# Attention decode kernel: K and V in units of eight heads and rows of 65536 B instead of units of two heads and rows of 49152 B

## The chip, the cores and the metric

The kernel runs on one core of one Trainium2 chip. The metric is the device time of one execution in microseconds, the median of three runs. Here and below the engines are called as the profile calls them: PE (matrix multiplication), PEld (its weight loads), DVE (vector engine), ACT (activation engine), POOL, and SP, which issues the large DMA transfers. A DMA transfer goes in rows, one contiguous run for each of the 128 partitions of on-chip memory.

## The reference

Two independent attention blocks, A and B, each decode one token for two batch entries with 32 heads of 192 dimensions over 8192 cached tokens. All arrays are bfloat16.

```python
def _A_ref(x, k_cache, v_cache, wq, wo):          # _B_ref computes the same
    q = (x @ wq).reshape(B, Sq, Hq, Dh).transpose(0, 2, 1, 3)
    scores = jnp.einsum("bhqd,bhkd->bhqk", q, k) * (Dh ** -0.5)
    p = _softmax(scores, axis=-1)
    o = jnp.einsum("bhqk,bhkd->bhqd", p, v)
    return o.transpose(0, 2, 1, 3).reshape(B, Sq, Hq * Dh) @ wo
return jnp.concatenate([a, b], axis=-1)
```

K and V of both blocks have 2 x 2 x 2 x 32 x 8192 x 192 elements of two bytes, 805.3 MB. The weights wq and wo of both blocks add 31.5 MB. Every byte is read once, and each is used in about one multiplication.

## The kernel before

The work is cut into **64 units** of two heads of one batch entry of one block (`NU`, L134). A unit's K is one DMA load of 6.29 MB (`ld_kv`, L264): partitions 0 to 63 hold the first head, 64 to 127 the second, 128 tokens on each partition, 49152 B in one row. A unit's V is another such load. SP issues them in the order of `loads` (L213): K of unit 0, then K of unit 1, V of unit 0, K of unit 2, V of unit 1 and so on. They go in turn into three buffers (`NBUF`, L137), so load i waits until the data of load i-3 has been used up (`done`, L485). For K that is the unit's last multiplication on DVE, for V its last matmul. Beside the three buffers, two small ones (`prod`, L183) hold products.

**Queries.** At the start PE multiplies x by wq for one pair of heads after the other (`pe_q`, L353), with x spread over 64 partitions for each batch entry, so that each query comes out copied to the 64 partitions that need it. DVE and ACT move them to `qall`, where the queries of all 64 units lie (L279 to L286).

**Scores.** A unit's K is taken in four pieces of 32 tokens. DVE multiplies a piece by the unit's query into a product buffer (`dve_mul`, L288). PE adds groups of 16 dimensions by twelve matmuls with the identity (`pe_sum`, L363), and DVE adds the 16 partial sums that are left (`dve_red`, L293). Then DVE takes each partition's maximum (L296), POOL the maximum over the partitions (`pool_ar`, L270), ACT makes the bias of it and the exponentials with their sums (`act_nb`, `act_exp`).

**Output of a unit.** PE multiplies the exponentials with V, 64 matmuls with two tokens each (`pe_pv`, L348), in the program's order after the sums of the next unit. DVE and ACT divide by the sum and put the result back into `qall` (L304 to L314).

**The order on each engine** is fixed by the slot and the number given to `put` (L423, L440 to L461); inside a loop over three units nothing moves. On DVE the first multiplication of unit 1 stands ahead of unit 0's last reduction (L443). **At the end** `pe_turn` brings the outputs into the layout of the projection, block A's while the last unit still runs, and `pe_out` multiplies with wo, which SP loads after the last V into buffers that are free by then (`pieces`, L227).

Of the kernel before, what the change touches and what calls it, by code (L numbers as in the profile page):

```python
# [5 lines left out]
ALU = mybir.AluOpType  # L6
# [110 lines left out]

def build_kernel(nc, blocks, out):
# [4 lines left out]
    T = Sk // 64  # L123
    TC = 32
    NCH = T // TC
    TJ = T // 2
# [4 lines left out]
    PPB = Hn // 2  # L131
    UPB = PPB * B
    NP = NBLK * PPB
    NU = NP * B  # L134
    LASTU = NU - 1
    scale = float(Dh) ** -0.5
    NBUF = 3  # L137
    MP = 34
    JB = 16
    QW = 2 * Dh  # L140
    BUFE = T * Dh
    PRODE = TC * Dh
    WR = Hn * Dh // 128
    GP = Dh // WR
    HP = 32

    with ExitStack() as es:
# [4 lines left out]
        rc = [sb(f"rc{i}", [2, 1], F32) for i in range(3)]  # L152
        o_hi = sb("o_hi", [2, Dh], F32)
        ones = sb("ones", [128, 1], F32)
        big = sb("big", [128, NBUF * BUFE + 2 * PRODE], BF16)
        qall = sb("qall", [128, NU, Dh], BF16)
        pb = [sb(f"pb{i}", [128, 2 * T], BF16) for i in range(3)]
        actd = sb("actd", [128, 2], F32)
        xw = sb("xw", [128, NBLK * DC * 128 + D], BF16)
        sc = [sb(f"sc{i}", [128, T], F32) for i in range(3)]  # L160
        mp = [sb(f"mp{i}", [128, 2], F32) for i in range(3)]
        mg = [sb(f"mg{i}", [128, 2], F32) for i in range(3)]
        nb = [sb(f"nb{i}", [128, 1], F32) for i in range(3)]
        rs = [sb(f"rs{i}", [128, 2], F32) for i in range(3)]
        ident = sb("ident", [128, 128], BF16)
        tri = sb("tri", [HP, HP + 1], BF16)
        place = sb("place", [2, 256], BF16)
        o_sum = sb("o_sum", [2, Dh], F32)
        oT = [sb(f"oT{k}", [128, WR, B], BF16) for k in range(NBLK)]
        out_sb = sb("out_sb", [HP + B, D], BF16)  # L170
        first = sb("first", [16, 128], BF16)

        ops = [ps(f"ops{i}", [128, 512], F32) for i in range(3)]
        scps = [ps(f"scps{i}", [128, TC, DG], F32) for i in range(3)]
        outps = ps("outps", [128, 512], F32)
        oTps = ps("oTps", [128, 512], F32)
        qbank = [t[:].rearrange("p a b -> p (a b)") for t in scps]
        oacc = [outps[:], qbank[(LASTU * NCH + 1) % 3]]
        qps = qbank + [outps[:]]
        NQ = len(qps)  # L180

        kv = [big[:, i * BUFE:(i + 1) * BUFE].rearrange("p (t d) -> p t d", d=Dh) for i in range(NBUF)]
        prod = [big[:, NBUF * BUFE + i * PRODE:NBUF * BUFE + (i + 1) * PRODE].rearrange("p (t d) -> p t d", d=Dh)  # L183
                for i in range(2)]
        WQE = DC * Hn * Dh
        wq_off = [BUFE, BUFE + WQE]
        assert BUFE + 2 * WQE == NBUF * BUFE + 2 * PRODE
        wq_t = [big[:, o:o + WQE].rearrange("p (c n) -> p c n", c=DC) for o in wq_off]

        XBE = NBLK * DC * 128  # L190
        xbc = xw[:, 0:XBE].rearrange("p (k c m) -> p k c m", k=NBLK, c=DC)
        x4 = xw[0:NBLK * B, XBE:XBE + D]

# [3 lines left out]
        S_act = _Stream("act", sem("s_act"), reg)  # L197
        S_dve = _Stream("dve", sem("s_dve"), reg)
        S_pool = _Stream("pool", sem("s_pool"), reg)
# [7 lines left out]
        wq_cut = [[(0, WQ0), (WQ0, DC * Hn * Dh)], [(0, DC * Hn * Dh)]]  # L207
# [3 lines left out]
        dsem(("first",))  # L211
# [6 lines left out]
        bcount = [0] * NBUF  # L218
        for i, (kind, u) in enumerate(loads):
            buf[kind, u] = i % NBUF  # L220
            bcount[i % NBUF] += 1
            reg[(kind, u)] = (bsem[i % NBUF], 16 * bcount[i % NBUF])

        bk, b62, b63 = buf["k", LASTU], buf["v", LASTU - 1], buf["v", LASTU]
        assert (bk, b62, b63) == (2, 0, 1)
        woA, wo0, wo1 = bk * BUFE, b62 * BUFE, b63 * BUFE
        pieces = []  # L227
        for blk, rows, off, w in ((0, (WR,), woA, [("s", LASTU, NCH - 1)]), (1, (29,), wo0, [("pv", LASTU - 1)]),
                                  (1, (11, 5, 2, 1), wo1, [("pv", LASTU)])):
            r = 29 if off == wo1 else 0  # L230
            for n in rows:
                pieces.append((blk, r, r + n, off, w))
                off, r, w = off + n * D, r + n, []
            assert r == (29 if off == wo0 + 29 * D else WR)
        NA = 0
        assert 29 * D <= BUFE and woA + WR * D <= NBUF * BUFE + 2 * PRODE
        for n in range(len(pieces)):
            dsem(("wo", n))

        def key(name, *idx):  # L240
            return (name,) + tuple(idx)

        def back(name, u, c, n):
            i = u * NCH + c - n
            return (name, i // NCH, i % NCH) if i >= 0 else None

# [17 lines left out]
        def ld_kv(kind, u):  # L264
            hp, b = u // B, u % B
            blk, h = hp // PPB, 2 * (hp % PPB)
            src = blocks[blk][kind][b, h:h + 2].rearrange("s (p t) d -> (s p) t d", p=64)
            return dma(kv[buf[kind, u]], src, (kind, u))

        def pool_ar(u):  # L270
            return lambda eng: eng.partition_all_reduce(mg[u % 3][:], mp[u % 3][:], 128, bass.bass_isa.ReduceOp.max)  # L271

        def dve_xbc(blk, b):
            src = oTps[:, 0:4 * DC].rearrange("p (c r) -> p c r", r=4)[:, :, B * blk + b:B * blk + b + 1]
            dst = xbc[:, blk, :, 64 * b:64 * b + 64]
            return lambda eng: eng.tensor_copy(dst, src.broadcast_to([128, DC, 64]))  # L276

        def dve_qx(hp, s):
            ri, ro = slice(64 * (1 - s), 64 * (1 - s) + 64), slice(64 * s, 64 * s + 64)  # L279
            return lambda eng: eng.tensor_copy(qall[ro, S_dve.at(B * hp + 1 - s, 1, B), :],  # L280
                                               qps[hp % NQ][ri, s * Dh:(s + 1) * Dh].unsqueeze(1))

        def act_q(hp, s):
            r = slice(64 * s, 64 * s + 64)
            return lambda eng: eng.activation(qall[r, S_act.at(B * hp + s, 1, B), :],  # L285
                                              qps[hp % NQ][r, s * Dh:(s + 1) * Dh].unsqueeze(1), ACTF.Identity)  # L286

        def dve_mul(u, c):  # L288
            t = kv[buf["k", u]]
            return lambda eng: eng.tensor_tensor(prod[c % 2], t[:, c * TC:(c + 1) * TC, :],  # L290
                                                 qall[:, S_dve.at(u), :].broadcast_to([128, TC, Dh]), ALU.mult)

        def dve_red(u, c):  # L293
            return lambda eng: eng.tensor_reduce(sc[u % 3][:, c * TC:(c + 1) * TC], scps[(u * NCH + c) % 3][:], AXL.X, ALU.add)  # L294

        def dve_max(u):  # L296
            def fn(eng):
                for s in range(2):
                    r = slice(64 * s, 64 * s + 64)
# [320 lines left out]
```

## Time and profile before

| what | value |
|---|---|
| median of three runs | 1937.0 us (1936.92 to 1937.27) |
| span of the profiled execution, first to last instruction | 1935.4 us |
| time of the profiled execution itself | not listed apart from its span, which lies 1.6 us under the median |
| PE busy | 1507.4 us, 78% of the span |
| DVE busy | 1123.0 us, 58% |
| ACT busy | 142.4 us, 7% |
| POOL busy | 28.6 us, 1% |
| moved by DMA | 836.92 MB, mean 432 GB/s |
| granted TensorE clock, mean | 0.952 |

The page gives each engine's busy time, a strip of 40 equal slices of the span with busy shares in tenths, the DMA queues, the chain of work that ended last, and the costliest groups of instructions. Beside the page, the trace answers by stage (windows), by instruction in order of time (timeline), and by who waited for whom.

### The profile page before, as it was taken

How to read it: one execution, taken by the hardware profiler on the slowest of the kernel's cores; microseconds unless marked ns; L12 is line 12 of the kernel's file. 1: busy time of each engine (PE TensorE's matmuls, PEld its weight loads, DVE VectorE, ACT ScalarE, POOL GpSimd, SP SyncE). 2: the span in 40 equal slices, each digit the busy share in tenths (PEclk: the TensorE clock that was granted, in tenths of full speed). 3: DMA queues.
4: the chain of work that ended last, by engine and by line, in shares of the span. 5: the costliest groups of instructions: out<-in, count | busy, mean ns of one | idle time of the engine just before them, and what ended most of it. 6: DMA issues, size and time to landing. Idle time of an engine off the chain costs nothing.

```text
span 1935.4 us, 19062 instructions
## 1 busy us (share of the span) xinstructions
PE 1507.4 (78%) x7729; PEld 732.1 (38%) x7729; DVE 1123.0 (58%) x907; ACT 142.4 (7%) x519; POOL 28.6 (1%) x113
## 2 busy tenths in 40 slices
PE   5777878878878878878878877877877877877878
PEld 2333433433433433434433433433433433433434
DVE  4765565565565565565565565565565565565560
ACT  3100000000000000000000000000000000000000
POOL 0000000000000000000000000000000000000000
PEclk9899999999999999999999999999999999999998
DMA  9999999999999999999999999999999999999999
GB/s 423 424 435 438 430 434 437 434 431 437 436 429 436 437 430 434 438 432 433 437 436 428 437 435 430 436 437 430 435 437 432 433 437 435 430 436 437 429 435 394
DMA packets 19786, 836.92 MB, mean 432 GB/s; under 512 B 2232, under 2 KB 2368, under 8 KB 2752
## 3 DMA queue, kind: packets, MB, share of 16 engines
q1 hardware_dynamic: 19744, 836.78, 99.9%
q8 instruction: 6, 0.10, 0.0%
q14 instruction: 4, 0.03, 0.0%
q10 hardware_dynamic: 32, 0.00, 0.0%
HBM read 836.77 MB, written 0.01 MB: 432 GB/s over the span
## 4 chain that ended last, share of the span: by engine, by line
DMA 49%; PE 29%; DVE 17%; issue 5%; DVEq 0%; SPq 0%; ACT 0%; ACTq 0%
DMA big<-in_B_k_cache_dram 25%; DMA big<-in_A_k_cache_dram 22%; PE ops L381 18%; DVE big L290 15%; PE scps L367 9%; DVE sc L294 2%; DMA big<-in_B_wo_dram 1%; PE scps L359 1%; DMA xw<-in_B_x_dram 1%; PE outps L359 0%; PE ops L373 0%; DVEq L290 0%; DVE qall L280 0%; PE scps L409 0%; SPq L249 0%
## 5 line engine op out<-in xcount | busy, mean ns | idle before, releaser
L290 DVE TENSOR_TENSOR big<-big,qall 128x6144 bf16<-128x6144 bf16 x256 | 852.8, 3352 | 522.0 <-DMA big<-in_B_k_cache_dram 275.3
L367 PE MATMUL scps<-big,ident 128*128 128x512 bf16 x3072 | 777.8, 411 | 395.3 <-DVE big L290 393.0
L381 PE MATMUL ops<-big,pb 128*34 128x384 bf16 x4096 | 676.8, 326 | 0.0
L367 PEld LDWEIGHTS scps<-big,ident 128*128 128x128 bf16 x3072 | 303.3, 104 | 863.1 <-DVE big L290 483.6
L381 PEld LDWEIGHTS ops<-big,pb 128*34 128x34 bf16 x4096 | 395.5, 98 | 258.7
L294 DVE TENSOR_REDUCE sc<-scps 128x32 f32<-128x512 f32 x256 | 176.0, 687 | 196.8 <-PE scps L367 196.8
L320 ACT ACTIVATE nb<-mg 64x1 f32<-64x1 f32 x128 | 25.7, 201 | 1707.1 <-POOL mg L271 1706.4
L329 ACT ACTIVATE pb<-sc,nb 64x128 bf16<-64x128 f32 x128 | 55.8, 436 | 7.8
L271 POOL PARTITION_ALL_REDUCE mg<-mp x64 | 25.9, 404 | 1857.9 <-DVE mp L300 1857.9
L300 DVE TENSOR_REDUCE mp<-sc 64x1 f32<-64x128 f32 x128 | 35.9, 280 | 8.3
L314 ACT ACTIVATE qall<-o_sum,rc 2x192 f32 (+1 forms) x64 | 29.0, 453 | 20.7 <-DVE o_sum L311 19.1
L311 DVE TENSOR_TENSOR o_sum<-ops,o_hi 2x192 f32<-2x192 f32 x64 | 22.1, 345 | 7.7
L359 PE MATMUL scps<-big,xw 128*128 x120 | 23.2, 351 | 2.2 <-DVE xw L276 2.2
L329 ACT ACTIVATION_READ_ACCUMULATOR pb<-sc,nb 64x1 f32 x128 | 23.7, 185 | 0.0
L308 DVE COPY o_hi<-ops 2x192 f32<-2x192 f32 x64 | 22.3, 349 | 2.0
L305 DVE RECIPROCAL rc<-ops 2x1 f32<-2x1 f32 x64 | 10.0, 156 | 21.3 <-PE ops L381 19.3
L280 DVE CAST qall<-scps 64x192 f32 x48 | 17.0, 355 | 6.5 <-PE scps L359 4.5
L285 ACT ACTIVATE qall<-scps 64x192 f32 x48 | 15.6, 325 | 29.4 <-DVE qall L280 27.2
L350 PE MATMUL oTps<-ident,xw 4*128 4x4 bf16 x5 | 0.4, 178 | 21.5 <-DMA xw<-in_B_x_dram 21.5
L359 PEld LDWEIGHTS scps<-big,xw 128*128 128x128 bf16 x120 | 12.4, 103 | 11.4 <-issue 5.2
L373 PEld LDWEIGHTS ops<-ones,rs 128*2 128x2 f32 x128 | 5.5, 82 | 26.9 <-issue 26.9
L409 PE MATMUL outps<-big,oT 128*2 128x320 bf16 x96 | 9.5, 375 | 5.5 <-DMA big<-in_A_wo_dram 5.5
(36 smaller groups left out, 67.9 us busy)
## 6 DMA issues: line engine op xcount, KB each, us to landing
big<-in_A_k_cache_dram SPq DMA_DIRECT2D x32, 6144.0 KB, 28.9
big<-in_A_v_cache_dram SPq DMA_DIRECT2D x32, 6144.0 KB, 27.9
big<-in_B_k_cache_dram SPq DMA_DIRECT2D x32, 6144.0 KB, 28.9
big<-in_B_v_cache_dram SPq DMA_DIRECT2D x32, 6144.0 KB, 27.9
big<-in_B_wq_dram SPq DMA_DIRECT2D x1, 7680.0 KB, 37.1
big<-in_A_wo_dram SPq DMA_DIRECT2D x1, 7680.0 KB, 30.0
big<-in_A_wq_dram SPq DMA_DIRECT2D x1, 7168.0 KB, 20.2
big<-in_B_wo_dram SPq DMA_DIRECT2D x1, 4640.0 KB, 30.3
```

Of the source, the lines that this page charges most:

```text
L271: return lambda eng: eng.partition_all_reduce(mg[u % 3][:], mp[u % 3][:], 128, bass.bass_isa.ReduceOp.max)
L290: return lambda eng: eng.tensor_tensor(prod[c % 2], t[:, c * TC:(c + 1) * TC, :], qall[:, S_dve.at(u), :].broadcast_to([128, TC, Dh]), ALU ...
L294: return lambda eng: eng.tensor_reduce(sc[u % 3][:, c * TC:(c + 1) * TC], scps[(u * NCH + c) % 3][:], AXL.X, ALU.add)
L300: ins = eng.tensor_reduce(mp[u % 3][r, s:s + 1], sc[u % 3][r, :], AXL.X, ALU.max)
L308: return lambda eng: eng.tensor_copy(o_hi[:], ops[u % 3][32:34, Dh:QW])
L311: return lambda eng: eng.tensor_tensor(o_sum[:], ops[u % 3][0:2, 0:Dh], o_hi[:], ALU.add)
L314: return lambda eng: eng.activation(qall[0:2, S_act.at(u), :], o_sum[:].unsqueeze(1), ACTF.Identity, scale=rc[u % 3][:])
L320: ins = eng.activation(nb[u % 3][r, :], mg[u % 3][r, s:s + 1], ACTF.Identity, scale=-scale)
L329: ins = eng.activation(dst, sc[u % 3][r, :].rearrange("p (g j a) -> p g a j", j=JB, a=2), ACTF.Exp, bias=nb[u % 3][r, :], scale=scale, acc ...
L359: ins = eng.matmul(qps[hp % NQ][:, 0:QW], xbc[:, blk, c, :], wq_t[blk][:, c, S_pe.at(off, QW, QW)], start=(c == 0), stop=(c == DC - 1))
L367: ins = eng.matmul(scps[(u * NCH + c) % 3][:], ident[:], prod[c % 2][:, :, j * DG:(j + 1) * DG], start=(j == 0), stop=(j == NJ - 1))
L381: ins = eng.matmul(ops[u % 3][0:MP, 0:QW], pb[u % 3][:, j0s:j0s + MP], vv[:, j, :], start=(j == 0), stop=(j == TJ - 1))
```

## The change

A unit is now **eight heads** of one batch entry of one block, 16 units in all. A unit's K is one contiguous stretch of 25.2 MB: each partition has a sixteenth of a head, 512 tokens or 196608 B, in three loads of 65536 B a row (`ROW`), 8.39 MB each. A load is called a chunk here; it holds 170 whole tokens of each partition and a fragment of 128 elements (chunks 0 and 2) or two of 64 (chunk 1), because 65536 B end amid a token. Loads go K and V in turn, chunk by chunk, but the three chunks of unit 0's K come first, one after the other. There are 96 loads in three buffers.

- The products overwrite K in its buffer, and the two product buffers are gone. A K buffer is free when PE's last sum over its chunk is done (`("sl", u, c)`), no longer when DVE's last multiplication is.
- A chunk is five pieces, four of 32 tokens and one of 42; PE's sums of the ten tokens over go to a bank `rest`, and the fragments' products to a small buffer `pad`, summed with the unit's last chunk.
- Queries: 80 matmuls for each block gather all heads of both batch entries on 64 partitions (`pe_proj`), and one pair of matmuls for each unit spreads the unit's eight queries to their partitions (`pe_q`), into a single buffer `qt`.
- Maximum, all-reduce and bias have eight columns, one for each head; the bias `nb` is made on DVE (`dve_nb`), not on ACT. Eight exponentials of 128x512 each write every eighth column of `pb`, with a mask so that each takes its own head's partitions.
- `sc`, `pb`, `mp`, `mg`, `nb`, `rs` and `ops` exist once, not three times.
- A unit's output is added to its rows of one PSUM bank (`pe_pl`), and both blocks are turned after the last unit.

```diff
-    T = Sk // 64
-    TC = 32
+    UH = 8
+    HG = Hn // UH
+    NU = NQB * HG
+    TP = Sk * UH // 128
+    NCH = 3
+    ROW = TP * Dh // NCH
+    TC = ROW // Dh
...
-        loads = [("k", 0)]
+        loads = [("k", 0, c) for c in range(NCH)]
         for u in range(1, NU):
-            loads += [("k", u), ("v", u - 1)]
-        loads += [("v", LASTU)]
+            for c in range(NCH):
+                loads += [("k", u, c), ("v", u - 1, c)]
+        loads += [("v", LASTU, c) for c in range(NCH)]
...
+        def dve_mul(u, c, k):
+            b = buf["k", u, c]
+            def fn(eng):
+                if k == 0:
+                    for t, lo, hi, src in fragments(b, c):
+                        eng.tensor_tensor(pad[:, t, lo:hi], src, qt[:, 0, lo:hi], ALU.mult)
+                t = tokens(b, c, SUB * k, size(k))
+                return eng.tensor_tensor(t, t, qt[:].broadcast_to([128, size(k), Dh]), ALU.mult)
...
+        def dve_nb(eng):
+            return eng.scalar_tensor_tensor(nb[:], mg[:], -scale, negm[:], ALU.mult, ALU.add)
...
+        def act_exp(eng):
+            src = sc[:].rearrange("p (g j a) -> p g a j", j=4, a=2)
+            for h in range(UH):
+                dst = pb[:].rearrange("p (g a j h) -> p g a j h", a=2, j=4, h=UH)[:, :, :, :, h]
+                ins = eng.activation(dst, src, ACTF.Exp, bias=nb[:, h:h + 1], scale=scale, accum_out=rs[:, h:h + 1])
...
+        def pe_q(eng):
+            eng.matmul(outps[:, 0:Dh], su[:, 16:144], qc[:, 0:Dh], start=True, stop=False)
+            return eng.matmul(outps[:, 0:Dh], su[:, 0:128], qc[:, Dh:QW], start=False, stop=True)
...
+        def pe_rest(u, c):
+            t = tokens(buf["k", u, c], c, SUB * NSUB, REST)
+            parts = [(REST * c, REST, t)] + ([(NCH * REST, 2, pad[:])] if c == NCH - 1 else [])
+            def fn(eng):
+                for lo, n, src in parts:
+                    for j in range(NJ):
+                        ins = eng.matmul(rest[:, lo:lo + n, :], ident[:], src[:, :, j * DG:(j + 1) * DG],
+                                         start=(j == 0), stop=(j == NJ - 1))
...
         def done(i):
-            kind, u = loads[i]
-            return ("m", u, NCH - 1) if kind == "k" else ("pv", u)
+            kind, u, c = loads[i]
+            return ("sl", u, c) if kind == "k" else ("pv", u, c)
...
+                put("dve", u, ("su", 1), dve_su(u + 1), [("q", u)])
+                for c in range(NCH):
+                    for k in range(NSUB):
+                        w = [("k", u, c), ("qe", u), ("sl", u - 1, NCH - 1) if u and c == 0 else None]
+                        put("dve", u, ("m", c, k), dve_mul(u, c, k), w)
+                        put("pe", u, ("s", c, k), pe_sum(u, c, k), [("m", u, c, k), prev(u, c, k)])
+                        if k:
+                            put("dve", u, ("r", c, k - 1), dve_red(u, c, k - 1),
+                                [("s", u, c, k - 1), ("exp", u - 1) if u else None])
+                    put("dve", u, ("r", c, NSUB - 1), dve_red(u, c, NSUB - 1), [("s", u, c, NSUB - 1)])
+                    put("pe", u, ("sl", c), pe_rest(u, c),
+                        [("m", u, c, NSUB - 1), ("rl", u - 1) if u and c == 0 else None])
+                    if c == NCH - 1:
+                        put("dve", u, ("rl",), dve_rest, [("sl", u, c)])
+                        put("dve", u, ("mx",), dve_max, [("rl", u)])
+                        put("dve", u, ("mp",), dve_mp, [("mx", u), ("ar", u - 1) if u else None, ("negm",)])
+                        put("dve", u, ("nb",), dve_nb, [("ar", u), ("exp", u - 1) if u else None])
+                        put("pool", u, ("ar",), pool_ar, [("mp", u), ("nb", u - 1) if u else None])
...
+                    if old:
+                        put("pe", u, ("pv", c, -1), pe_pv(v, c), [("v", v, c)])
...
+                put("act", u, ("exp",), act_exp, [("nb", u), ("pv", v, NCH - 1) if u else None])
...
+        S_dve.add(dve_oall(0), waits=[("pl", LASTU), ("q", NU)], sig=("oa", 0))
+        S_dve.add(dve_oall(1), sig=("oa", 1))
+        for blk in range(NBLK):
+            S_pe.add(pe_turn(blk), waits=[("oa", blk), ("rl", LASTU), ("r", LASTU, NCH - 1, NSUB - 1)], sig=("t", blk))
```

In each engine's stream the names mean: `m` multiply a piece, `s` sum it on PE, `r` reduce it on DVE, `sl` the sums of the tokens over, `rl` their reduction, `mx` and `mp` the maximum, `ar` the all-reduce, `nb` the bias, `exp` the exponentials, `l` and `pv` their product with V.

SP's stream shows which waits stand ahead of the first loads (rows of an engine's instructions in order; a wait in brackets). Before:

```order
L249 DMA big<-in_A_k_cache_dram 128x24576
L249 DMA big<-in_A_k_cache_dram 128x24576 [waits s_pe]
L249 DMA big<-in_A_v_cache_dram 128x24576 [waits s_pe]
L249 DMA big<-in_A_k_cache_dram 128x24576 [waits s_dve]
L249 DMA big<-in_A_v_cache_dram 128x24576 [waits s_dve]
```

and now:

```order
L253 DMA big<-in_A_k_cache_dram 128x32768
L253 DMA big<-in_A_k_cache_dram 128x32768 [waits s_pe] x3
L253 DMA big<-in_A_v_cache_dram 128x32768 [waits s_pe]
L253 DMA big<-in_A_k_cache_dram 128x32768 [waits s_pe]
L253 DMA big<-in_A_v_cache_dram 128x32768 [waits s_pe]
```

Two K loads stood at the head, and a V load came third; now four K loads stand at the head (unit 0's three chunks and unit 1's first), and every later load waits for PE, where K's had waited for DVE.

On DVE, the end of unit 0 and the start of unit 1, before (`mp` is the maximum):

```order
L290 TENSOR_TENSOR big<-big,qall 128x6144 [waits bsem1]
L294 TENSOR_REDUCE sc0<-scps0 128x32 [waits s_pe]
L300 TENSOR_REDUCE mp0<-sc0 64x1 [waits s_pool,s_dve]
L300 TENSOR_REDUCE mp0<-sc0 64x1
L290 TENSOR_TENSOR big<-big,qall 128x6144
L294 TENSOR_REDUCE sc1<-scps1 128x32 [waits s_pe]
```

and now (`rest` holds the sums of the tokens over):

```order
L310 TENSOR_REDUCE sc<-scps2 128x32 [waits s_pe]
L314 TENSOR_REDUCE sc<-rest 128x3x10 [waits s_pe]
L315 TENSOR_REDUCE sc<-rest 128x2
L318 TENSOR_REDUCE rmax<-sc 128x1 [waits s_dve]
L321 TENSOR_SCALAR mp<-negm,rmax 128x8 [waits s_dve]
L324 SCALAR_TENSOR_TENSOR nb<-mg,negm 128x8 [waits s_pool]
L292 TENSOR_TENSOR su<-esel,onehot 128x144 [waits s_pe]
L300 TENSOR_TENSOR pad<-big,qt 128x128 [waits s_act,bsem0]
L302 TENSOR_TENSOR big<-big,qt 128x6144 x2
L310 TENSOR_REDUCE sc<-scps0 128x32 [waits s_act,s_pe]
```

Unit 1's first multiplication stood ahead of unit 0's last reduction and its maximum; now it stands behind both and behind the bias, which waits for POOL. Unit 1's first reduction now waits for ACT's exponentials too, since `sc` exists once.

More of the change, by code (lines that the diff above doesn't have):

```diff
@@ L161, in build_kernel @@
[L161 to L170, printed above, removed]
@@ L278, in dve_qx @@
[L278 to L286, printed above, removed]
```

514 lines of the change are left out of this document (272 added, 242 removed).

## The prediction

> **What bounds the kernel now.** First the page's strips and queues, then windows of the middle, then the chain of work that ended last.
>
> ```profile
> span 1935.4 us, 19062 instructions
> DMA  9999999999999999999999999999999999999999
> GB/s 423 424 435 438 430 434 437 434 431 437 436 429 436 437 430 434 438 432 433 437 436 428 437 435 430 436 437 430 435 437 432 433 437 435 430 436 437 429 435 394
> q1 hardware_dynamic: 19744, 836.78, 99.9%
> ```
>
> The DMA strip never leaves 9, and SP's queue keeps the 16 DMA engines busy for 99.9% of the span. The bytes set the time. Windows (length, busy time and count of PE, PEld, DVE, ACT, POOL, granted clock, DMA share, GB/s) show one steady rate:
>
> ```profile
> 100.00:500.00 400.00, 318.29 (x1583) 153.30 (x1582) 238.69 (x182) 25.92 (x98) 4.99 (x14) 0.94 1.00 434
> 1700.00:1900.00 200.00, 157.86 (x871) 77.89 (x871) 114.50 (x93) 13.66 (x51) 2.49 (x7) 0.97 1.00 435
> ```
>
> PE is busy 80% here and DVE 60%; neither is the bound while the next load is issued in time. Two entries of the chain, four loads apart, give a load's price:
>
> ```profile
> 1578.03 3.18 issue
> 1636.04 3.16 issue
> ```
>
> 58.01 us for four loads is 14.50 us each. Four old loads are 25.17 MB, exactly three new ones, so a new load should take **19.34 us**. Any stretch in which no load is under way now lengthens the kernel by its whole length; work on an engine costs nothing until it delays a load.
>
> **The DMA stream.** The bytes stay. 128 K and V loads become 96, and a load has a small price beyond its bytes. In the last pieces of wo, weight loads waiting for DMA show landings:
>
> ```profile
> 1932.16 0.50 PEld L409 LDWEIGHTS scps<-big,oT 128*2 128x2 bf16 x10 [0.54 <-DMA big<-in_B_wo_dram]
> 1932.93 0.09 PEld L409 LDWEIGHTS scps<-big,oT 128*2 128x2 bf16 x4 [0.27 <-DMA big<-in_B_wo_dram]
> 1933.33 0.08 PEld L409 LDWEIGHTS scps<-big,oT 128*2 128x2 bf16 x2 [0.31 <-DMA big<-in_B_wo_dram]
> ```
>
> The piece of two rows took 0.77 us and that of one row 0.40, so a row is 0.37 and the rest 0.03. 32 loads fewer save **1.0 us**. Bounds of the rate: 438 GB/s, the page's best slice, would take 17 us off the 1856 us of K and V; 428, its lowest middle one, would add 26.
>
> The Trainium skill, "DMA: Bandwidth & Descriptors", section "Anatomy of one DMA — SWDGE (gpsimd) path", puts a fixed 2.0 us plus bytes at 436 GB/s on each SWDGE DMA. If every load here paid it in turn, 32 fewer would give 1873 us. The period of 14.50 us leaves no room for it: it is hidden behind the load under way.
>
> **The first unit.** A load may start when load i-3 is used up, so three loads always wait or run, and a K chunk has two load times, 38.7 us, before its buffer stalls the queue. In the middle that is enough (below). At the start it isn't, because four K loads come back to back and DVE needs more than 19.34 us for each. The prices, from the timeline (start, length, engine, line, operation, count, idle before and releaser) and from the chain:
>
> ```profile
> 58.55 5.29 PE scps L367 x12
> 63.86 0.69 DVE L294 TENSOR_REDUCE sc<-scps 128x32 f32<-128x512 f32 x1 [2.15 <-PE scps L367]
> 64.47 3.35 DVE L290 TENSOR_TENSOR big<-big,qall 128x6144 bf16<-128x6144 bf16 x1
> 67.74 0.68 DVE L294 TENSOR_REDUCE sc<-scps 128x32 f32<-128x512 f32 x1
> 67.88 2.76 PE L367 MATMUL scps<-big,ident 128*128 128x512 bf16 x12 [1.32 <-DVE big L290]
> 68.34 3.35 DVE L290 TENSOR_TENSOR big<-big,qall 128x6144 bf16<-128x6144 bf16 x1
> 76.94 3.42 POOL L271 PARTITION_ALL_REDUCE mg<-mp  x1 [73.70 <-DVE mp L300]
> 93.38 0.36 POOL L271 PARTITION_ALL_REDUCE mg<-mp  x1 [13.01 <-DVE mp L300]
> 98.62 6.63 DVE L290 TENSOR_TENSOR big<-big,qall 128x6144 bf16<-128x6144 bf16 x2 [5.33 <-DMA big<-in_A_k_cache_dram]
> 1001.35 7.04 PE L367 MATMUL scps<-big,ident 128*128 128x512 bf16 x24 [3.48 <-DVE big L290]
> ```
>
> A multiplication holds DVE 3.27 us (64.47 to 67.74), a reduction 0.60; 42 tokens are 3.27 x 42/32 = 4.29. A sum on PE takes 2.76 us, after 5 us of idle PE 5.29, and after 3.48 us idle 1.5 more (7.04 against 5.52 for two). A fragment's product is priced by 32x32 elements:
>
> ```profile
> L519 DVE TENSOR_TENSOR ident<-tri 32x32 bf16<-32x32 bf16 x4 | 0.7, 165 | 2.1 <-POOL tri L511 2.1
> ```
>
> A chunk is then: fragment 0.15, two multiplications, a reduction, two times 3.87, 4.29, the last sum, 2.76 (a reduction fits beside it), and the last reduction 0.6: **22.7 us**, plus what a slow first sum adds, and 0.1 to 0.3 for handovers.
>
> 1. The fourth K or V load of before landed at 98.6; the first was 3 x 14.50 earlier, at 55.1, and the first chunk now lands 4.84 later, at **59.9**. The next land every 19.34: 79.3, 98.6, 117.9 (unit 1's first), V 137.3, 156.6.
> 2. Chunk 0: 59.9 + 25.1, with a first sum of 5.29, ends at 85.0. Chunk 1, 24.1 with a sum after 3.3 us idle: 109.1. Chunk 2: 131.8, its last PE sum at 131.1. It landed at 98.6: DVE is already 10 us late.
> 3. Unit 0's end, in which DVE does nothing else. PE's sums of the tokens over (24 small matmuls, 2.3 us): 133.4. Two reductions of 480 and 32 inputs, a maximum of 512 and the mask follow on DVE; by the 0.69 of a reduction of 512 inputs that is 1.4 to 2.8, and I take 1.7, as two of them are small: 135.1. The first all-reduce, 3.42 like its row (the 63 others take 0.36): 138.6, since `nb` stands on DVE behind it. Two small operations, 0.25 each: 139.1.
> 4. Unit 1, chunk 0: first multiplication to 142.5; PE has idled since 133.7, so the sum takes about 5.0 (between 2.76 + 1.5 and 5.29), to 147.5; the exponentials (8 x 0.82) end at 145.5 and just hide. First reduction to 148.2, two times 3.87, 4.29, sum 2.76, ten tokens over 1.3: **164.3**.
> 5. The load behind it, V's second chunk, is issued only now. An unqueued load lands 2.5 us late beyond its bytes:
>
> ```profile
> big<-in_A_wq_dram SPq DMA_DIRECT2D x1, 512.0 KB, 3.7
> ```
>
> 3.7 less 1.2 for 0.52 MB at 434 GB/s. It lands at 164.3 + 2.5 + 19.34 = 186.1; without a gap it would be 175.9. **The DMA engines idle 10.2 us once.** The two steps before come out closer: unit 1's second chunk waits for 133.4 and is needed by about 134.
>
> Unseen costs. Small matmuls: the nearest rows are 24 ns (64 of two partitions and 96 or 192 columns in 1.51 us) and 230 (512 columns); at 36 of them on the path that is 0.9 to 8.3 us, and I take 3.6, nearer the small ones by size. The exponentials of 512:
>
> ```profile
> 1895.65 1.51 PE L395 MATMUL oTps<-qall,place 2*32 2x96 bf16 x64
> 1018.53 0.44 ACT L329 ACTIVATE pb<-sc,nb 64x128 bf16<-64x128 f32 x1
> 1019.04 0.43 ACT L329 ACTIVATE pb<-sc,nb 64x128 bf16<-64x128 f32 x1
> L342 ACT ACTIVATE out_sb<-outps 2x320 bf16<-2x320 f32 x1 | 0.4, 427 | 14.7 <-PE outps L409 14.7
> L285 ACT ACTIVATE qall<-scps 64x192 f32 x48 | 15.6, 325 | 29.4 <-DVE qall L280 27.2
> ```
>
> Two of 128 start 0.51 apart. From 192 to 320 elements ACT adds 102 ns, 0.8 ns each; 384 more are 0.31: 0.82. Bounds are 0.51 and four times that, 2.04; at the start only what exceeds 1.05 shows, up to 8 us; below 1.7 nothing else does but a few us of tail. Products in place: same shape, type and step as before, so I take the old price; the floor is that too, the ceiling is a rival. The queries are no term: 160 projection matmuls stay 160, and the last query, for which the first multiplication waited until 55.09, comes before 59.9 still:
>
> ```profile
> 55.09 6.63 DVE L290 TENSOR_TENSOR big<-big,qall 128x6144 bf16<-128x6144 bf16 x2 [1.00 <-ACT qall L285]
> ```
>
> The 4 KB load on ACT's queue goes; only the last output waited for it.
>
> **The middle.** PE for a pair of loads: 5 x 2.76 + 1.3 + 85 x 0.165.
>
> ```profile
> 1016.14 10.57 PE L381 MATMUL ops<-big,pb 128*34 128x384 bf16 x64
> ```
>
> 10.57/64 is 0.165, so V's chunk takes 14.1 and the pair 29.2 of 38.7. A K chunk is released 24 us after it lands (27 for a unit's first), where 36 is needed; V lands 19.3 after K, starts on PE at 24, ends at 38.4, which is 19 after landing. DVE needs 21 of 38.7. At a unit's turn the exponentials wait for V's last chunk at 38.4 and end at 46.5, when the next unit's second multiplication ends too. The bias is ready by 28, so a slower all-reduce or the bias on DVE costs nothing there; on DVE the end of V's last chunk stands ahead of the next unit, some 3 us late, which is the 27. So about 10 us or more of cover remain everywhere, and the late start is caught up within two units, at no gain.
>
> **The tail.** Block A's projection used to be ready early and waited for wo:
>
> ```profile
> 1915.15 9.46 PE L409 MATMUL outps<-big,oT 128*2 128x320 bf16 x96 [5.53 <-DMA big<-in_A_wo_dram]
> ```
>
> Now it follows the last unit: 3.5 us more of matmuls with V (14.1 against 10.57) and about 2.4 for turning both blocks, against 5.53 of cover. **0.4 us** later; 0 to 6 if the last exponentials are late.
>
> **Sum.** 1935.4 - 1.0 + 10.2 + 0.4 = 1945.0 of span; the runs' median lies 1.6 above the span of before: **1946.6 us**, 0.5% slower.
>
> **Rivals.**
> - *No dry queue:* the chain of step 4 ends before 154. It needs 10.2 us less: a quick first all-reduce (-3.1), no slow sums (-6), cheaper small matmuls (-2.7). Time 1936.4. Against it: all these rows stand in this trace's start. Chance 0.15, with stalls under 5 us counted here.
> - *Standing stalls:* exponentials that write with a step of eight, or slower products, use up the 10 us of cover in every unit. Late exponentials also push V's matmuls and with them the next sums on PE, so I put the point near 1.7 us each. At 2.04 it is 8 x 0.34, some 3 us, in 15 units, 8 at the start and 10 at the tail: about 2010. Products at twice the time put 17 us on each K chunk, 5 over its 12 of cover, at least 48 x 5 more: above 2180. Chance 0.11.
> - *Rows 196608 B apart read worse:* 428 GB/s throughout adds 26 us: 1973. The rows show no such effect for 49152 B, nor exclude it. Chance 0.07. The Trainium skill, "DMA: Bandwidth & Descriptors", section "Latency and other measured facts", has copies at row pitches of large powers of two slower (207 against 214 GB/s at 512 KiB); by that figure 1856 us would grow by 63, an estimate. This pitch is three times 64 KiB, and no run here shows it yet.
> - *A better rate:* 438 GB/s, 1930. Chance 0.03, as the middle windows hold 434 and 435.
>
> **How the numbers follow.** The forecast, 1941 to 1956, has 0.64. A measurement of this kernel tells 0.2%, 3.9 us, from no change: faster 0.03 (better rate), same 0.15 (no dry queue), slower 0.82. The forecast's own range takes small matmuls and exponentials at their bounds; the range of 8 in 10, 1937 to 1962, adds most of the first rival and the low part of the second.
>
> **What would show it.** One hole in the DMA strip near 160 us and none later; SP waiting for PE's sums of unit 1's chunk 0 near 164; DVE working almost without waits for DMA from 60 to 160; the first all-reduce about 3.4 us with DVE idle; then waits for DMA on DVE in every unit. A rate under 433 GB/s in the middle, or DVE multiplications longer than 3.35 us, would make the forecast wrong, and so would a strip without a hole.

## The result, and the profile after

| | before | after | predicted |
|---|---|---|---|
| median | 1936.99 us | 2032.72 us (2029.35 to 2035.06) | 1946.6 us (1937 to 1962) |
| profiled span | 1935.4 us | 2029.9 us | 1945.0 us |
| ratio | | 1.0493 [1.0478, 1.0508] | 1.0050 |

The kernel is slower, as forecast, but by 95.7 us instead of 9.6; the time lies outside the range. First the page of the kernel after: its span, the strip of DMA with the rate of each fortieth, SP's queue, and the chain of work that ended last.

```profile
span 2029.9 us, 18563 instructions
DMA  9996999999999998999999999999999999998997
GB/s 414 434 432 271 432 399 434 435 389 434 393 434 413 434 434 372 434 393 434 434 413 434 393 434 393 434 434 393 434 393 434 393 434 434 413 434 372 434 434 311
q1 hardware_dynamic: 15136, 836.78, 95.8%
PE 54%; DVE 24%; ACT 13%; issue 6%; DMA 2%; another core or an unknown queue 0%; ACTq 0%; SPq 0%; DVEq 0%; POOL 0%
```

The hole in the fourth slice is the one that was forecast. The rest was not: every second or third slice falls from 434 to between 372 and 413, and ACT, which had 0% of this chain in the kernel before, holds 13% of it. The windows of after (columns as in the prediction) show the start, and that a stage in the middle no longer runs at the old rate:

```profile
100.00:200.00 100.00, 65.62 (x330) 30.59 (x329) 67.66 (x43) 18.86 (x17) 0.36 (x1) 0.88 0.81 344
500.00:900.00 400.00, 299.30 (x1566) 150.39 (x1567) 218.38 (x142) 75.24 (x70) 1.10 (x3) 0.90 0.96 414
```

The costliest groups by line name what ACT does there (busy time, mean ns of one, idle time before and its releaser):

```profile
L302 DVE TENSOR_TENSOR big<-big,qt 128x6144 bf16<-128x6144 bf16 (+1 forms) x240 | 848.1, 3550 | 0.0
...
L310 DVE TENSOR_REDUCE sc<-scps 128x32 f32<-128x512 f32 x240 | 165.2, 688 | 532.1 <-PE scps L407 355.2
L352 ACT ACTIVATE pb<-sc,nb 128x512 bf16<-128x512 f32 x128 | 295.7, 2722 | 2.0 <-DVE nb L324 2.0
```

An exponential lasts 2.72 us and overlaps with the next one, which begins 2.28 us after it (second fence below). That distance is what compares with the prediction's 0.82, whose highest bound was 2.04. The multiplications in place kept their price: 3.35 us for 32 tokens, 4.35 for 42, 3.55 as a mean. The timeline of unit 0's end and unit 1's start, and of the same place one unit later, first DVE, then ACT, then SP. An exponential begins every 2.28 us (the second after 2.10), so eight take 18.2:

```profile
137.38 0.17 DVE L324 SCALAR_TENSOR_TENSOR nb<-mg,negm 128x8 f32<-128x8 f32 x1 [0.57 <-POOL mg L327]
...
137.82 6.62 DVE L302 TENSOR_TENSOR big<-big,qt 128x6144 bf16<-128x6144 bf16 x2
156.22 0.69 DVE L310 TENSOR_REDUCE sc<-scps 128x32 f32<-128x512 f32 x1 [11.78 <-ACT pb L352]
...
243.12 0.17 DVE L324 SCALAR_TENSOR_TENSOR nb<-mg,negm 128x8 f32<-128x8 f32 x1 [0.49 <-POOL mg L327]
255.24 0.15 DVE L330 RECIPROCAL rc<-ops 8x1 f32<-8x1 f32 x1 [11.95 <-PE ops L437]
...
275.06 0.69 DVE L310 TENSOR_REDUCE sc<-scps 128x32 f32<-128x512 f32 x1 [12.02 <-ACT pb L352]
```

```profile
137.59 2.58 ACT L352 ACTIVATE pb<-sc,nb 128x512 bf16<-128x512 f32 x1 [1.96 <-DVE nb L324]
...
139.69 2.76 ACT L352 ACTIVATE pb<-sc,nb 128x512 bf16<-128x512 f32 x1
...
141.97 2.76 ACT L352 ACTIVATE pb<-sc,nb 128x512 bf16<-128x512 f32 x1
...
256.55 2.56 ACT L352 ACTIVATE pb<-sc,nb 128x512 bf16<-128x512 f32 x1
```

```profile
293.05 0.33 SPq L253 DMA_DIRECT2D big<-in_A_v_cache_dram  x1
```

DVE has done two multiplications of unit 1 by 144.4. Its first reduction writes `sc`, which the exponentials are still reading, so it waits for them 11.78 us; in unit 2 (275.06) it waits 12.02. Behind it on DVE stand the other three multiplications of that K chunk, behind those PE's sums over it, and behind them, on SP, the load that needs this chunk's buffer: V's second chunk. In the later units the exponentials also begin late, since `pb` exists once and PE must first be done with V of the unit before: unit 1's bias is ready at 243.3, PE's last product ends at 255.2, the exponentials begin at 256.55, the reduction at 275.06, and SP issues V's second chunk at 293.05. A second `sc` or `pb` may be another remedy; neither was tried.

In what follows a **hole** is how much longer than 19.33 us passes between the landings of two successive K and V loads, read from the trace's DMA packets. A load counts as landed with the 124th of its 128 rows, because the last rows lag by as much as 2 us. If the last row is taken instead, single holes change by up to 1.8 us (V's second chunk of unit 0 has 17.7), but the sums hardly do (20.8 at the start, 63.1 later). The 94.5 us between the two spans are then, within 0.2:

| | us |
|---|---|
| start: unit 1's second K chunk 1.2, V's second chunk of unit 0 19.45 | 20.6 |
| V's second chunk of each later unit, 14 holes of 3.0 to 6.0 | 64.2 |
| wo's first piece lands 21.9 after the last V chunk instead of 18.8 | 3.1 |
| from there to the end, 27.9 instead of 21.1 | 6.8 |

The last two rows together are called the **tail** below: from the landing of the last V chunk to the end, 39.9 us before and 49.8 after.

### The profile page after: what moved, and what is told of

Read it like the earlier page. It is cut to its first block, busy times and chain, and to the rows that moved or that the text cites. A ratio compares the mean times of both kernels' runs of the same rounds, so it can differ in the third digit from the quotient of the medians.

```text
span 2029.9 us, 18563 instructions
## 1 busy us (share of the span) xinstructions
PE 1528.0 (75%) x8255; PEld 781.9 (39%) x8256; DVE 1048.6 (52%) x723; ACT 311.4 (15%) x300; POOL 8.9 (0%) x61
## 4 chain that ended last, share of the span: by engine, by line
PE 54%; DVE 24%; ACT 13%; issue 6%; DMA 2%; another core or an unknown queue 0%; ACTq 0%; SPq 0%; DVEq 0%; POOL 0%
PE ops L437 33%; DVE big L302 21%; PE scps L407 16%; ACT pb L352 13%; DVE sc L310 3%; PE rest L419 2%; DMA big<-in_B_wq_dram 2%; PE scps L389 1%; PE ops L443 0%; PE outps L471 0%; PE scps L471 0%; DVE o_hi L333 0%; DVE o_hi L336 0%; PE ops L425 0%
## 5 line engine op out<-in xcount | busy, mean ns | idle before, releaser
L407 PE MATMUL scps<-big,ident 128*128 128x512 bf16 x2880 | 746.9, 419 | 432.2 <-DVE big L302 432.2
L302 DVE TENSOR_TENSOR big<-big,qt 128x6144 bf16<-128x6144 bf16 (+1 forms) x240 | 848.1, 3550 | 0.0
L437 PE MATMUL ops<-big,pb 128*40 128x384 bf16 x4080 | 682.3, 327 | 0.0
L437 PEld LDWEIGHTS ops<-big,pb 128*40 128x40 bf16 x4080 | 404.7, 100 | 255.6 <-issue 4.8
L352 ACT ACTIVATE pb<-sc,nb 128x512 bf16<-128x512 f32 x128 | 295.7, 2722 | 2.0 <-DVE nb L324 2.0
L330 DVE RECIPROCAL rc<-ops 8x1 f32<-8x1 f32 x16 | 2.5, 155 | 243.3 <-PE ops L437 243.3
L352 ACT ACTIVATION_READ_ACCUMULATOR pb<-sc,nb 128x1 f32 x128 | 63.0, 492 | 0.0
L419 PEld LDWEIGHTS rest<-big,ident 128*128 128x128 bf16 x576 | 44.5, 101 | 13.2 <-issue 3.3
L419 PE MATMUL rest<-big,ident 128*128 128x160 bf16 x576 | 49.2, 237 | 0.0
L389 PE MATMUL scps<-big,pb 128*64 128x384 bf16 x160 | 29.1, 348 | 1.6 <-DMA big<-in_B_wq_dram 1.1
L449 PE MATMUL oall<-o_sb,place 8*128 8x192 bf16 x16 | 4.0, 249 | 25.2 <-ACT o_sb L339 25.2
L381 PE MATMUL rest<-ident,pb 4*128 4x4 bf16 x5 | 0.4, 178 | 21.9 <-DMA pb<-in_B_x_dram 21.9
L327 POOL PARTITION_ALL_REDUCE mg<-mp x16 | 5.8, 366 | 1923.5 <-DVE mp L321 1923.5
## 6 DMA issues: line engine op xcount, KB each, us to landing
big<-in_B_wo_dram SPq DMA_DIRECT2D x1, 4640.0 KB, 18.8
```

The costliest lines, as they stand in the source:

```text
L302: return eng.tensor_tensor(t, t, qt[:].broadcast_to([128, size(k), Dh]), ALU.mult)
L327: return eng.partition_all_reduce(mg[:], mp[:], 128, bass.bass_isa.ReduceOp.max)
L352: ins = eng.activation(dst, src, ACTF.Exp, bias=nb[:, h:h + 1], scale=scale, accum_out=rs[:, h:h + 1])
L389: ins = eng.matmul(flat[blk][64 * blk:64 * blk + 64, 0:QW], xz[:, blk, c, XM - m:XM - m + 64], wq_t[blk][:, c, QW * m:QW * m + QW], start= ...
L407: ins = eng.matmul(scps[bank(u, c, k)][:], ident[:], t[:, :, j * DG:(j + 1) * DG], start=(j == 0), stop=(j == NJ - 1))
L419: ins = eng.matmul(rest[:, lo:lo + n, :], ident[:], src[:, :, j * DG:(j + 1) * DG], start=(j == 0), stop=(j == NJ - 1))
```

## The experiments

**e1: what makes an exponential slow.** The eight exponentials of a unit in eight forms over 256 of its 512 tokens; the output lacks the other half.

```diff
-            for h in range(UH):
-                dst = pb[:].rearrange("p (g a j h) -> p g a j h", a=2, j=4, h=UH)[:, :, :, :, h]
+            forms = [(steprun(0, 8, 0, 4), run(4)), (step(0, 8, 1), flat), ...
+                     (pb[:, 2304:2560], flat), (step(2560, 2, 0), flat), ...
+                     (step(3072, 4, 0), flat), (steprun(3072, 4, 1, 4), run(4))]
+            for h, (dst, src) in enumerate(forms):
```

> The eight exponentials of a unit take eight forms over 256 tokens each, half of the 512 of the changed kernel, so the output lacks the other half. Forms in order: step 8 (16 B) in runs of 4; step 8 without runs; contiguous out, read in runs of 4; contiguous both; step 2 without runs; step 2 in runs of 16 (as before the change); step 4 without runs; step 4 in runs of 4. Now 512 elements take 2.72 us and start 2.28 apart. Theory 'step': the step of 16 B on the written side makes them long; then forms 1 and 2 start about 1.3 us apart from the next and forms 3 to 6 about 0.6, step 4 between. Rival 'runs': the inner run of four does it; then forms 1, 3 and 8 are long and 2, 4, 5, 7 short. Rival 'neither' (the bias of masked partitions, the accumulation, a busy memory): all eight alike, about 1.3.

The timeline of ACT in e1, in the order of the forms: the first two write with a step of eight elements, the third and fourth contiguously, the fifth with a step of two, and the last row is the seventh, with a step of four. The first, third and eighth form read in runs of four, the sixth in runs of sixteen, the others straight through.

```profile
137.78 1.43 ACT L363 ACTIVATE pb<-sc,nb 128x256 bf16<-128x256 f32 x1 [1.96 <-DVE nb L324]
...
138.74 1.61 ACT L363 ACTIVATE pb<-sc,nb 128x256 bf16<-128x256 f32 x1
...
139.88 0.69 ACT L363 ACTIVATE pb<-sc,nb 128x256 bf16<-128x256 f32 x1
...
140.56 0.49 ACT L363 ACTIVATE pb<-sc,nb 128x256 bf16<-128x256 f32 x1
...
141.05 0.57 ACT L363 ACTIVATE pb<-sc,nb 128x256 bf16<-128x256 f32 x1
...
142.10 0.85 ACT L363 ACTIVATE pb<-sc,nb 128x256 bf16<-128x256 f32 x1
```

From start to start: 1.14 with a step of eight (0.95 after the first of the series), 0.65 with four, 0.52 with two, 0.49 contiguous (the 0.69 of the third still holds the end of the second). How the input is read makes no difference: the fifth and sixth form, both with a step of two, take 0.52 each. 1.14 us for 256 elements and 2.28 for 512 are the same 4.45 ns each: the **step of the write** is the cause. One run, 1947.8 us, holes of 1.4 and 7.2 at the start and none after unit 1.

**e2: contiguous exponentials, all else as after.** The products with V read the weights of other tokens, so the output is not the reference's.

```diff
-                ins = eng.activation(dst, src, ACTF.Exp, ...)
+                ins = eng.activation(pb[:, TP * h:TP * h + TP], sc[:], ACTF.Exp, ...)
```

> The eight exponentials read and write 512 contiguous elements (the order of the exponentials in memory is then wrong for V's matmuls, nothing is left out). Theory 'exponentials': they are the whole of the standing stalls; each then takes about 0.75 us, the DMA engines idle once, 6 to 9 us before V's second chunk of unit 0, never again, and the time is 1940 to 1947. Rival 'other cause' (PE's order, DVE's single buffers, slower DMA): holes of 3 to 6 us stay in each unit and the time stays above 2000.

The group of e2's exponentials, and two of its windows:

```profile
L350 ACT ACTIVATE pb<-sc,nb 128x512 bf16<-128x512 f32 x128 | 90.3, 705 | 2.0 <-DVE nb L324 2.0
```

```profile
100.00:200.00 100.00, 73.43 (x382) 35.21 (x383) 71.27 (x45) 6.08 (x17) 0.36 (x1) 0.93 0.94 400
500.00:1900.00 1400.00, 1114.78 (x5986) 567.72 (x5984) 761.30 (x505) 77.10 (x216) 4.38 (x12) 0.94 1.00 434
```

1946.0 us (ratio 1.0046 [1.0029, 1.0063]), one hole of 6.8 us at V's second chunk of unit 0, none above 0.6 later, 434 GB/s in the middle. With exponentials of 0.71 us the kernel does what the prediction said, to 0.6 us. That the time agrees so closely is partly luck: two terms of the sum were off against each other (below).

**e3: one exponential, spread by DVE.** Each partition holds one head, so one exponential in place does, and DVE spreads it over eight columns by a mask (two instructions, 4.49 us). DVE writes all eight columns side by side, so this does not test the rival that a step of eight slows DVE too.

```diff
+            return eng.activation(sc[:], sc[:], ACTF.Exp, bias=nb1[:], scale=scale, accum_out=rs1[:])
...
+            for a in range(2):
+                eng.tensor_tensor(out[:, :, a], src[:, :, a].unsqueeze(3).broadcast_to(...), mask..., ALU.mult)
```

> One exponential of 512 elements in place for each unit, with each partition's own bias, and two DVE multiplications by the heads' mask (2048 products each, some 2.2 us) that write the step of eight. Theory 'exponentials': exponentials and spreading take some 5.5 us of each unit instead of 18.8, so no hole after the first unit; the spreading stands on DVE in the first unit's chain, so the one hole is 9 to 13 us: 1944 to 1951. Rival 'step hurts every writer': the DVE multiplications take over 4 us each as well, holes come back in the units, above 1960.

1955.5 us (1.0097 [1.008, 1.0113]): no standing holes, but 12.6 us at the start, since unit 1's first multiplication now waits behind the spread (142.20 instead of e2's 136.51). It is 4 us over what was expected, with the hole in its range: smaller holes of 1.5 in all, the loads' own 1.7 (below) and a tail 1.9 longer than before's come on top. Here 5.7 us of work put on DVE ahead of unit 1 made the hole 5.8 longer.

**e6 and e7: how long may a unit's exponentials be?** Part of the tokens is written with a step of eight, the rest contiguously (`N` = 256 and 384 of 512).

```diff
+                eng.activation(pb[:, 0:N * UH].rearrange("p (s h) -> p s h", h=UH)[:, :, h], sc[:, 0:N], ACTF.Exp, ...)
+                ins = eng.activation(pb[:, N * UH + (TP - N) * h:N * UH + (TP - N) * (h + 1)], sc[:, N:TP], ACTF.Exp, ...)
```

> Each head's exponential in two: 256 tokens written with a step of eight, 256 contiguous (the products with V read weights of other tokens for these). By e1 that is 1.14 + 0.49 = 1.63 us a head, 13.0 a unit, just under 8 x 1.7 = 13.6. Theory (only the length of a unit's exponentials counts, and the point is 13.6): no hole after unit 1, or under 0.6 us each; the hole at the start 5.1 us longer than e2's 6.8, about 12; 1950 to 1955. Rival (the point lies lower, or a write with a step of eight disturbs PE or the loads by itself): holes of 1.5 us and more in every unit, over 1970.

> As e6, with 384 tokens written with a step of eight and 128 contiguous: 1.71 + 0.39 = 2.10 us a head, 16.8 a unit, 3.2 over 13.6. Theory: holes of about 3.2 us in each of 14 units, 45 in all, 15 to 17 at the start, and a tail some 5 longer than e2's: 1995 to 2010. Rival (holes come in some other way from the length, for example all at once above a threshold): 4.5 us a unit and over 2020, or under 1 and 1960.

| | a unit's exponentials, us | hole at V's second chunk of unit 0 | holes after unit 1, sum | time, us |
|---|---|---|---|---|
| e2 | 8 x 0.70 = 5.6 | 6.8 | 0.5 | 1946.0 |
| e6 | 8 x 1.64 = 13.1 | 14.6 | 1.3 | 1957.9 |
| e7 | 8 x 2.06 = 16.5 | 18.5 | 48.5 | 2014.3 |
| after | 8 x 2.28 = 18.2 | 19.45 | 64.2 | 2032.7 |

Windows of the same stretch, first e6, then e7:

```profile
500.00:900.00 400.00, 321.19 (x1695) 161.82 (x1696) 228.69 (x148) 41.36 (x102) 1.10 (x3) 0.93 1.00 433
```

```profile
500.00:900.00 400.00, 307.00 (x1608) 154.84 (x1609) 220.07 (x143) 65.09 (x130) 1.10 (x3) 0.90 0.97 419
```

At 13.1 us the middle still runs at 433 GB/s. At 16.5 each of 14 units has a hole of 3.3 to 3.7, mean 3.46; at 18.2 the mean is 4.59. If a unit pays us for us behind the point, these put it at 13.0 and 13.6 us, 1.63 to 1.70 for one exponential, and e6's small holes agree; the prediction had 1.7. That a unit pays us for us is not shown: between e7 and after themselves 1.7 us more cost 1.1. Both kernels, one run each, came out 3 and 4 us over the expected range: the hole at the start is 1.5 to 2.6 longer than expected, and in e7 the standing holes are 3.5 more in all. The tail grows too: 39.8 us in e2, 42.5 in e6, 48.6 in e7.

**e4: the hole at the start.** Contiguous exponentials as in e2, and DVE takes the first multiplication of chunks 1 and 2 ahead of the last reduction of the chunk before.

```diff
+                    if c < NCH - 1:
+                        put("dve", u, ("m", c + 1, 0), dve_mul(u, c + 1, 0), [("k", u, c + 1), ("qe", u)])
                     put("dve", u, ("r", c, NSUB - 1), dve_red(u, c, NSUB - 1), [("s", u, c, NSUB - 1)])
```

> Contiguous exponentials as in e2 (products with V read weights of other tokens), and DVE takes the first multiplication of chunk 1 and of chunk 2 ahead of the last reduction of the chunk before. Theory (the hole that e2 has left, 6.8 us at V's second chunk, is DVE's own chain of the first unit: in e2 DVE waits 3.94 and 2.26 us for the last sums of chunks 0 and 1): both waits go, the hole falls to 0 to 1.5 us, and the time from e2's 1946.0 to 1939.5 (1938.5 to 1941). Rival (the hole is held by something else than these waits: the end of the exponentials, PE, or the loads): it stays at 6 to 7 us and the time at 1945 to 1947.

The last reduction of chunk 0 on DVE, first in e2, then in e4:

```profile
85.86 0.69 DVE L310 TENSOR_REDUCE sc<-scps 128x32 f32<-128x512 f32 x1 [3.94 <-PE scps L405]
```

```profile
81.69 0.28 DVE L300 TENSOR_TENSOR pad<-big,qt 128x64 bf16<-128x64 bf16 x2
81.89 3.35 DVE L302 TENSOR_TENSOR big<-big,qt 128x6144 bf16<-128x6144 bf16 x1
85.16 0.69 DVE L310 TENSOR_REDUCE sc<-scps 128x32 f32<-128x512 f32 x1
```

The wait is filled. The hole falls from 6.8 to 1.7 us (by the last row, from 5.3 to 0.4), the time to 1941.5 (1.0023 [1.0014, 1.0032]). Both lie a little above what was expected, the time by 0.5; the tail is 1.5 longer than e2's. The hole was DVE's chain, as the prediction's steps had it.

**e5: e4's order, and the spread where DVE waits.** The one exponential writes a free bank of PSUM; DVE spreads it in three parts, each ahead of a chunk's last reduction.

```diff
+            return eng.activation(ex[:], sc[:], ACTF.Exp, bias=nb1[:], scale=scale, accum_out=rs1[:])
...
+                        put("dve", u, ("sp", c, -1), dve_sp(c), [("exp", v), ...])
```

> Same output as the kernel after. One exponential of 512 tokens writes a bank of PSUM that was free, and DVE spreads it over the eight heads by a mask in three parts, each where DVE waits for a chunk's last sum (about 1.6 us each, from 4.49 for the whole in e3, in a wait of 2.26); the early multiplications of e4 are kept. Theory (the exponentials of 2.28 us and DVE's waits at the start are all that the kernel after lost, and the loads' rate is that of before): a hole of 0 to 1.5 us at the start, none later, a tail of 1 to 3 us, 1936 to 1940 us, no difference from before that 0.2% would show. Rival (the spread on DVE, or fewer and larger loads, cost something of their own): holes in every unit or a time over 1944.

1942.5 us (1.0028 [1.0016, 1.0039]): holes of 1.6 and 1.0 and no standing ones, but 2.5 us over the expected range, so my expectation of no difference from before was wrong. The 5.6 us of span over before are about 2.6 of holes, 1.9 of loads that each take a little longer (next section) and 1.1 of tail.

**e8: which writes are slow.** Four forms, two of each, over 256 or 128 tokens.

```diff
+            forms = [(runs(one, 4, 32, 0, H), src(4, H)), (runs(one, 4, 32, 4, H), src(4, H)),
+                     (runs(two, 2, 16, 0, H), src(2, H)), (runs(two, 2, 16, 2, H), src(2, H)),
+                     (runs(two, 1, 16, 4, Q), src(1, Q)), (runs(two, 1, 16, 5, Q), src(1, Q)),
+                     (runs(one, 16, 128, 8, H), src(16, H)), (runs(one, 16, 128, 40, H), src(16, H))]
```

> The eight exponentials of a unit in four forms, two of each, over 256 tokens (the third pair over 128), so the output lacks half. Which distance makes the write slow? e1: 256 tokens with a step of eight 1.14 us, of four 0.65, of two 0.52, contiguous 0.49. Theory P (each piece of 16 bytes that is written costs some 4.45 ns, however many elements it holds): runs of four elements, one in each 64 bytes (64 pieces), 0.5 us; runs of two, one in each 32 bytes (128 pieces), 0.57; a step of sixteen over 128 tokens (128 pieces), 0.57; runs of sixteen 0.5. Theory L (each stretch of 64 bytes costs some 18 ns): 1.14 for the runs of four, 1.14 for the runs of two, 1.14 for the step of sixteen, 0.5 to 0.6 for the runs of sixteen. Theory S (only a step between neighbours inside a run counts, and jumps between runs are free): 0.5 for all runs, more than 0.57 for the step of sixteen. The kernel as a whole near e1's 1947.7, with one hole of 7 us at the start.

The timeline of ACT in e8: the second run of four, the second run of two, and the two with a step of sixteen.

```profile
140.94 0.49 ACT L364 ACTIVATE pb<-sc,nb 128x256 bf16<-128x256 f32 x1
...
141.93 0.51 ACT L364 ACTIVATE pb<-sc,nb 128x256 bf16<-128x256 f32 x1
...
142.42 0.83 ACT L364 ACTIVATE pb<-sc,nb 128x128 bf16<-128x128 f32 x1
...
142.81 1.00 ACT L364 ACTIVATE pb<-sc,nb 128x128 bf16<-128x128 f32 x1
```

Runs of four, one in each 64 bytes, go at the contiguous price, 0.49, and so do the runs of sixteen. Theory L falls. Single elements 32 bytes apart begin 0.54 us apart for 128 (0.39 after the first of the two; the pair holds ACT 1.11), 4.2 to 4.4 ns each, about as at 16 bytes. Runs of two in each 32 bytes take 0.50 where P wanted 0.57, and e1's step of four takes 0.65 where P would have 0.57, so P is not exact either. S has all the runs right, but expected more than 0.57 for the step of sixteen. What the runs show is 4.2 to 4.5 ns for a single element whose neighbour is 16 bytes away or more, 2.5 at 8 bytes, and next to nothing once two or four lie side by side. Its mechanism stays open.

The kernel as a whole took 1950.3 us (one run), 2.6 more than expected, with 3.7 and 7.8 us of holes at the start instead of one of 7. In its trace PE's sums in unit 0 came later, and the bias at 140.2 instead of e2's 136.1; this part of the kernel differs from trace to trace.

**e9 and e10: the same kernel with runs of four.** Of a head's weights four tokens lie side by side; two tokens that share a matmul with V are sixteen apart. e10 adds e4's order.

```diff
+                ins = eng.activation(pb[:].rearrange("p (b h j) -> p h b j", h=UH, j=4)[:, h], ...)
...
+            j0 = 32 * (s // 4) + s % 4
+            return pb[:, j0:j0 + 4 * n - 3:4]
```

> Same output as the kernel after, same instructions on ACT, and the same order everywhere; only the place of the weights in pb is another: a head's four tokens lie side by side, the next four 64 bytes on, so that each exponential writes runs of four elements; on PE two tokens that share a matmul are sixteen apart (five in a chunk's last ten), and the stationary operand is read with a step of four. Theory (the write with a step of eight is the whole of the standing stalls, and it is the write of single elements 16 bytes apart that costs): exponentials of 0.70 to 0.75 us, no hole after unit 1, one of 6 to 8 us at the start, 1945 to 1948 us. Rival (what e2 gained came from the wrong weights or the missing spread, or PE pays for a stationary operand with a step): PE's weight loads grow over 0.1 us, V's chunks are released later, holes in every unit, over 1955.

> e9 with the early first multiplications of e4. Theory: both repairs add up; hole at the start 0 to 2 us, none later, 1939 to 1942.5 us, 0.1 to 0.3% behind before. Rival (the early multiplication in a loop of its own costs later): time as e9's or more.

A window of e9, two of its groups, and the group of after that the second compares with, in the last row:

```profile
500.00:1900.00 1400.00, 1119.73 (x5983) 612.29 (x5984) 764.55 (x519) 77.12 (x216) 4.39 (x12) 0.95 1.00 434
```

```profile
L352 ACT ACTIVATE pb<-sc,nb 128x512 bf16<-128x512 f32 x128 | 90.3, 705 | 2.0 <-DVE nb L326 2.0
...
L442 PEld LDWEIGHTS ops<-big,pb 128*40 128x40 bf16 x4080 | 460.0, 114 | 203.3 <-issue 4.5 <-DMA big<-in_B_v_cache_dram 1.1
```

```profile
L437 PEld LDWEIGHTS ops<-big,pb 128*40 128x40 bf16 x4080 | 404.7, 100 | 255.6 <-issue 4.8
```

e9 takes 1948.4 us (1945.67 to 1954.80; ratio 1.006 [1.0048, 1.0073]), with a hole of 9.6 in the profiled run, where 6 to 8 were expected, and no standing one later; the median is 0.4 over the expected range. Why its runs spread over 9 us is not shown, as only one was traced. The number of exponentials, their order and what they compute are those of after: the layout of `pb`, with the order of reading that follows from it, is worth 84 us. A stationary operand read with a step of four costs 114 ns instead of 100 (`LDWEIGHTS`, the last two rows), which PE absorbs. e10 takes 1941.2 us (1.0024 [1.0014, 1.0035]), level with e4, with a hole of 1.0. No version tried beats the kernel before.

## Why the prediction was wrong

- **The step that failed is the price of an exponential**: 0.82 us, bounds 0.51 and 2.04, against 2.28. Its start, 0.51, came from exponentials of 128 elements written with a step of two, and its price an element, 0.8 ns, from copies of 192 and 320. That the new write has a step of eight was named in a rival, but no row that the prediction used shows such a write, and the ceiling of four times the low bound was no bound.
- *Standing stalls* was therefore what happened, and its mechanism and its point were right: late exponentials hold DVE's first reduction, K's first chunk, and so V's second load; the point lies at 1.63 to 1.70 us, if us for us. By the rival's own formula, 8 x (2.28 - 1.7) = 4.6 us in each unit; measured 4.59 as a mean of 3.0 to 6.0. That this agrees so closely is partly luck, for e7 by the same formula would have 2.9 and had 3.46. The rival's 10 us of tail, reckoned for 2.04, are 9.9, and its 8 at the start 12.6 (19.45 - 6.8). It had a chance of 0.11.
- **The hole at the start**: right in place and cause (e4), 10.2 against 6.8 us in e2. The first all-reduce was taken at 3.42, and is no slower than the others: all sixteen have a mean of 366 ns (row below, of after). Why the first one of the kernel before took 3.42 is open. In e2 the bias is ready at 136.2 instead of 139.1, which is most of the difference.

```profile
L327 POOL PARTITION_ALL_REDUCE mg<-mp x16 | 5.8, 366 | 1923.5 <-DVE mp L321 1923.5
```

- **32 fewer loads, -1.0**: the sign was wrong. Four thirds of the old 14.500 us are 19.333, so nothing could be saved, and in the kernels without standing holes (e2, e4, e5, e9, e10) a load lands every 19.350 to 19.352 (median), which over 96 loads is 1.7 us more. With the hole 3.4 us shorter and the loads 2.7 longer than predicted, e2 ended near 1946.6.
- *Rows that read worse*: not so. e2's middle runs at 434 GB/s, as before.
- *Products in place* at the old price: right. The 0.4 of the tail: right to half a us without the slow exponentials (39.8 us in e2, 39.9 before).

## What to carry to other kernels

Price an instruction by its access pattern as well as by its count: before a layout is chosen for the reader (here PE's weights), look at the writer's innermost step. For the bf16 exponentials that ACT writes here, two or four elements side by side were enough; other writers were not tested. Where an unseen price enters eight times in a chain whose slack is known, the question is how far it is from the point where the slack ends, and a factor of two there decides the forecast. A wait for the last result of one piece can be filled with the first work of the next, if that has landed.

## What the hardware showed that I had not expected

An exponential of 128x512 from fp32 to bf16 starts every 0.71 us when it writes contiguously or in runs of four, and every 2.28 us with a step of eight (16 bytes), 4.45 ns an element. The Trainium skill, "ScalarE: Activation LUTs", section "What ACT_TABLE_LOAD costs", puts an ACTIVATE with a bias by pointer at about 280 ns and 0.833 ns an element, 707 ns for 512, an estimate by its figure. The rows of e2 and e9 (705 ns) agree; those of after (2722) do not, so that figure holds for contiguous writes and not for this one.

A load of 8.39 MB takes 19.35 us (median from last row to last row 19.350 to 19.356 in all the kernels with such loads, 19.352 in the one after), while the smaller loads of before took 14.500, three quarters of 19.333. Fewer and larger loads saved nothing; why 0.018 us a load come on top is open, and nothing was run to settle it.
